# Reordering the first batch's attention steps ahead of the first FFN group

## The chip, the cores and the metric

The kernel runs on one NeuronCore of a Trainium2 chip. The metric is the device time of one launch in microseconds (us). Five runs of the kernel before are given, and one more execution was recorded by the hardware profiler. Engines are named as in the profile: PE (matmul), PEld (weight load), ACT, DVE, POOL (which also issues most loads), SP (which issues stores and DMA transposes).

## The reference

Two operations are fused. The first is a masked attention over `q`, `k`, `v` of shape 8 x 8 x 576 x 64 (batch, head, position, head dimension). The second is a feed-forward network with a squared ReLU on the 4608 x 512 result.

```python
scores = scale * np.matmul(q, k.transpose(0, 1, 3, 2))       # B=8, H=8, S=576, D=64
mask_plain = (rel >= 0) & (rel < 32)                          # heads 0..3
mask_dil = (rel >= 0) & (rel < 128) & (rel % 4 == 0)          # heads 4..7
attn = softmax(where(mask, scores, -1e9));  attn_out = attn @ v
x = attn_out.transpose(0, 2, 1, 3).reshape(4608, 512)
h = np.maximum(x @ w_in, 0.0)                                 # w_in 512 x 2048
out = (h * h) @ w_out                                         # w_out 2048 x 512
```

## The kernel before

**Data.** The order of work is written by hand (a manual schedule): each engine runs its instructions in the order in which the program issues them, and each instruction waits on semaphores for its operands and its buffers. Heads are handled in pairs e = 0..3. Pairs 0 and 1 have the plain window and pairs 2 and 3 the dilated one. The result of attention goes, transposed, into `xT`, whose four slabs (one per pair) are the four contraction tiles of the first FFN product. A batch of 576 tokens is cut into two parts for batches 0 and 1: part 0 is tokens 0 to 255, part 1 is tokens 256 to 575.

**FFN.** It runs in groups. The first 1024 tokens are in tiles of 256 tokens, the rest in tiles of 512. Every tile has groups of `w_in` products (PE line L665, then a Relu on ACT at L676 and a square on DVE at L677) and groups of `w_out` products (PE L700, then a copy on ACT at L706 and a store on SP at L639). `w_in` comes in four transfers of 512 columns each (in the text w_in 0 to w_in 3) and so does `w_out` (w_out 0 to w_out 3). POOL issues all of these. For the first tile, group 0 does the products of pairs 0 and 1 for two accumulators, group 1 the products of pairs 2 and 3 for the same two, and groups 2 and 3 use w_in 1.

**The order.** The string `PROGRAM` lists the attention steps. Everything ahead of its first `|` runs before FFN group 0, what stands between the first and the second `|` runs after group 0, and so on. A first-batch step is a letter, a pair and a part, and `first_step` carries it out:

- `T` transposes q and k of a pair on PE (L497, 8 instructions for q and 8 for k) into a PSUM tile of pool `ps_a`, which has two buffers.
- `C` copies that tile to SBUF (`xx`). For the plain pairs it is L511 for q and L512 for k; for the dilated pairs L504 for both and L506 for the rest of k. The last letter says which engine does L504 or L511: `a` is ACT, `v` is DVE; L506 and L512 are always on DVE.
- `B` and `S` are the bias and the score products (PE, L527 and L546) in a tile of pool `ps_f`, which has four buffers. The FFN accumulators use the same four.
- `E` is the exponential (ACT, L554), in part 1 followed by a mask multiplication (DVE, L557).
- `P` and `D` are the products with v (PE L584) and with ones (PE L600). Their results are in `ps_o` and `ps_d` (pair of tiles po and pd), in two tiles of `ps_f`, or in two of `ps_a`.
- `L` and `X` are the logarithm and the exponential of its negative on ACT (L607, L610), which make the reciprocal of the sum. `M` is the multiplication on DVE that writes `xT` (L617). In part 0, one L, X and M serve two pairs.
- `W`n is a run of n small products on zeros (PE L467), whose results nobody reads.

Steps with a leading `L` and a batch number (`L1:q00123`) issue loads on POOL; `z`, `y`, `u`, `m`, `n` and `h` are memsets, masks and a copy of v. Steps of later batches start with the batch number: `3k1` and `3q1` copy the transposed k and q of batch 3, pair 1, from `xx` (k on DVE at L252, q on ACT at L248), and `L3:x` issues the four DMA transposes (SP, L216) that fill `xx` for batch 3.

**What orders the queues.** POOL's loads are in program order, and an issue on POOL often waits for the landing of an earlier transfer. SP's queue holds stores and DMA transposes in program order as well.

Of the kernel before, what the change touches and what calls it, by code (L numbers as in the profile page):

```python
# [20 lines left out]
PROGRAM = (  # L21
    "L0:q001 L0:q023 L0:q101 L0:q123 L0:v0d L0:i0 L0:v1dr L0:i1 L0:v1p L0:i2 L0:i3 L0:o0 L0:o1 L0:o2 L0:o3 "
    "L1:q00123 z y L1:v0dp L1:q10123 L1:v1dpr w9 T00 C00a T10 C10a B00 B10 W2 S00 E00 B20 W1 S10 E10 u B30 W3 "
    "T20q W6 T20k C20v T30 C30v h W3 S20 E20 W2 S30 E30 T01 C01v T11 C11v W2 P00 P10 D00 D10 L00 X00 M00 P20 "
    "P30 D20 D30 L20 X20 M20 S01 T21 C21a T31 C31v E01 S11 E11 | S21 E21 | S31 E31 P21 P31 D21 D31 L21 X21 M21 "
    "L31 X31 M31 | | P01 P11 D01 D11 L01 X01 M01 L11 X11 M11 | | | | | | | | | | | | | m n | | | | | L2:q00123 "
    "L2:q10123 | 1q1 1q3 | 1q2 1k2 | 1k1 1v3 | 1a2 | 1v2 1k0 1q0 | 1o2 | 1a0 1a1 | 1k3 1o0 1o1 | 1a3 1Q0 | 1K0 "
    "1o3 | 1Q1 1K1 | 1Q2 | 1b0 | | 1Q3 1K2 L2:vwpdr L3:q00123 L3:q10123 | L2:x | | 2q0 | | 2k0 1V2 | 1b2 1p0 | "
# [847 lines left out]
```

## Time and profile before

| | us |
|---|---|
| median of 5 runs | 313.53 (313.09 to 316.47) |
| profiled execution | 313.28 |
| its span, first to last instruction | 311.5 |
| PE busy in the span | 302.0 (97%) |
| ACT busy | 197.3 (63%) |
| DVE busy | 195.5 (63%) |
| POOL busy | 93.8 (30%) |

The time of the profiled execution is 1.78 us more than its span. A timeline row gives start, duration, engine, line, operation, output and inputs, the count of merged instructions, and in brackets the idle time before it with what ended it. A row of a tile gives the durations as minimum, median and maximum, the first and last start, and below it the time from issue to landing of its DMAs. PE's records overlap, since matmuls are pipelined, so the time that a run of matmuls takes is read from the start of one row to the start of the next.

### The profile page before, as it was taken

To read this page: it belongs to the slowest core of one execution; us is meant where nothing else is said; L and a number is where in the kernel's file an instruction comes from. 1 tells how busy PE (TensorE), PEld (TensorE's weight loads), DVE (VectorE), ACT (ScalarE), POOL (GpSimd) and SP (SyncE) were. 2 spreads that over 40 slices of the span, in tenths; PEclk is the share of its full clock that TensorE was granted. 3 is DMA by queue.
4 is the path that set the end of the run, shared out by engine and by line. 5 is a ranking of instruction groups with operands and counts; after the bars stand their busy time and mean duration, and the time that the engine had idled before them with its cause. 6 is when DMAs were issued, how large, how long until landed. Compare 5 with 4: busy or idle time off the path is not lost.

```text
span 311.5 us, 6788 instructions
## 1 busy us (share of the span) xinstructions
PE 302.0 (97%) x2564; PEld 186.4 (60%) x2564; DVE 195.5 (63%) x637; ACT 197.3 (63%) x421; POOL 93.8 (30%) x138
## 2 busy tenths in 40 slices
PE   8889999999999999999999999999999999999994
PEld 3679746969755555555599555555555555445443
DVE  1456667998978879975798469946994234104400
ACT  6578538859878865795388547854786456226511
POOL 8689775464236255401451041000000000000000
PEclk9999999999999999999999999999999999999999
DMA  7999999999999979998799976502200210121022
GB/s 112 193 173 213 204 141 176 174 97 225 151 123 192 177 115 203 167 147 131 106 129 147 142 120 91 102 16 61 60 3 4 66 68 0 36 67 34 2 67 67
DMA packets 79808, 35.04 MB, mean 113 GB/s; under 512 B 49824, under 2 KB 74784, under 8 KB 79776
## 3 DMA queue, kind: packets, MB, share of 16 engines
q0 software_dynamic: 46592, 18.23, 51.7%
q1 hardware_dynamic: 32496, 16.06, 27.9%
q10 hardware_dynamic: 688, 0.33, 0.5%
q8 instruction: 20, 0.33, 0.4%
q14 instruction: 12, 0.10, 0.1%
HBM read 36.90 MB, written 9.44 MB: 149 GB/s over the span
## 4 chain that ended last, share of the span: by engine, by line
PE 84%; ACT 5%; DMA 4%; DVE 3%; POOL 2%; issue 2%; SPq 0%; ACTq 0%; POOLq 0%
PE pf L665 37%; PE pf L700 37%; PE po L413 3%; DMA w_in<-in_moe_w_in_dram 3%; PE pd L415 2%; PE pa L304 2%; ACT h2T L676 1%; PE pa L310 1%; ACT qT L248 1%; PE pa L235 1%; POOL qb L161 1%; POOL kb L161 1%; DMA out_dram<-osb 1%; DVE xT L428 1%; ACT rec L417 1%
## 5 line engine op out<-in xcount | busy, mean ns | idle before, releaser
L700 PE MATMUL pf<-w_out_sb,h2T 128*128 128x512 bf16 (+1 forms) x592 | 134.5, 373 | 0.5 <-ACT osb L706 0.5
L665 PE MATMUL pf<-xT,w_in 128*128 128x256 bf16 (+1 forms) x768 | 133.8, 326 | 1.0 <-DMA w_in<-in_moe_w_in_dram 0.4
L665 PEld LDWEIGHTS <-w_in 128*128 128x128 bf16 x768 | 82.3, 114 | 36.4 <-issue 1.2
L676 ACT ACTIVATE h2T<-pf 128x512 bf16<-128x512 f32 x144 | 83.6, 597 | 23.2 <-PE pf L665 22.6
L700 PEld LDWEIGHTS <-h2T 128*128 128x128 bf16 x592 | 54.3, 98 | 53.9 <-issue 0.7
L677 DVE TENSOR_TENSOR h2T<-h2T 128x512 bf16<-128x512 bf16 x144 | 58.0, 422 | 38.4 <-ACT h2T L676 36.7
L706 ACT COPY osb<-pf 128x512 f32<-128x512 f32 (+1 forms) x37 | 21.2, 572 | 43.6 <-PE pf L700 41.3
L428 DVE TENSOR_TENSOR xT<-po,rec 128x288 bf16<-128x288 f32 (+2 forms) x52 | 23.7, 456 | 31.5 <-ACT rec L418 31.1
L178 POOL DMA_DIRECT2D vbd<-in_v_dram x36 | 25.7, 729 | 45.9 <-PE pd L415 40.0
L417 ACT ACTIVATE rec<-pd 128x288 f32<-128x288 f32 (+2 forms) x52 | 21.5, 413 | 24.0 <-PE pd L415 22.9
L314 ACT ACTIVATE pt<-pa 128x352 bf16<-128x352 f32 (+6 forms) x56 | 27.6, 499 | 8.4 <-PE pa L310 4.7
L418 ACT ACTIVATE rec<-rec 128x288 f32<-128x288 f32 (+2 forms) x56 | 24.8, 444 | 1.8
L413 PEld LDWEIGHTS <-vbd 128*128 128x128 bf16 x286 | 16.8, 97 | 9.9 <-issue 0.7
L248 DVE COPY qT<-xx 64x288 bf16<-64x288 bf16 x80 | 19.6, 246 | 1.1
L191 POOL DMA_DIRECT2D vd<-in_v_dram x24 | 14.7, 621 | 15.3 <-DMA kb<-in_k_dram 8.7
L252 DVE COPY kbd<-xx 64x288 bf16<-64x288 bf16 x40 | 18.8, 470 | 0.6
L413 PE MATMUL po<-pt,vbd 128*128 128x96 bf16 (+3 forms) x263 | 18.0, 199 | 0.3 <-DVE vbd L207 0.2
L161 POOL DMA_DIRECT2D qb<-in_q_dram x18 | 12.9, 718 | 17.8 <-DMA xx<-qb 16.2
L415 PE MATMUL pd<-pt,mk 128*128 128x96 bf16 (+5 forms) x158 | 16.3, 204 | 0.0
L197 POOL DMA_DIRECT2D vbd<-in_v_dram x16 | 9.6, 603 | 13.0 <-PE pd L415 5.1
L161 POOL DMA_DIRECT2D kb<-in_k_dram x18 | 12.7, 707 | 0.8 <-DMA kb<-in_k_dram 0.5
L304 PE MATMUL pa<-qT,kbd 128*128 128x96 bf16 (+2 forms) x146 | 12.2, 201 | 0.5 <-ACT qT L248 0.5
(90 smaller groups left out, 234.3 us busy)
## 6 DMA issues: line engine op xcount, KB each, us to landing
out_dram<-osb SPq DMA_DIRECT2D x18, 128.0 KB, 2.7
qb<-in_q_dram POOLq DMA_DIRECT2D x7, 320.0 KB, 8.3
kb<-in_k_dram POOLq DMA_DIRECT2D x7, 320.0 KB, 10.1
vd<-in_v_dram POOLq DMA_DIRECT2D x32, 64.0 KB, 7.2
w_in<-in_moe_w_in_dram POOLq DMA_DIRECT2D x4, 512.0 KB, 7.4
w_out_sb<-in_moe_w_out_dram POOLq DMA_DIRECT2D x4, 512.0 KB, 12.4
qb<-in_q_dram POOLq DMA_DIRECT2D x7, 256.0 KB, 7.0
kb<-in_k_dram POOLq DMA_DIRECT2D x7, 256.0 KB, 8.2
```

The costliest lines, as they stand in the source:

```text
L161: nc.gpsimd.dma_start(t[0:n, part, hs, :], src[b, hs, t0 : t0 + RES * n, :].rearrange("h (p r) d -> p h (r d)", r=RES))
L178: nc.gpsimd.dma_start(dst[rows, e, i0:i1, rows], v[b, 2 * e + hl, 64 * i0 : 64 * i1, :].rearrange("(i p) d -> p i d", p=64),)
L248: copy(qT[rows, e, :, m0 : m0 + n].rearrange("p (c j) m -> p j c m", j=2)[:, jj, :, :], src)
L314: nc.scalar.activation(pt[:, off : off + n], ps[:, 0:n], ACT.Exp, scale=SCALE)
L413: nc.tensor.matmul(oo, vb[:, e, i, :], rh, start=(x == 0), stop=(x == len(mms) - 1), skip_group_check=True)
L417: nc.scalar.activation(rec[:, 0:n], d[:, 0:n], ACT.Ln)
L418: nc.scalar.activation(rec[:, 0:n], rec[:, 0:n], ACT.Exp, scale=-1.0)
L428: nc.vector.tensor_tensor(out=tok, in0=o if o is o3 else o[:, 0:n], in1=rec if o is o3 else rec[:, 0:n], op=ALU.mult)
L665: nc.tensor.matmul(acc[u][:, nt * x + y0 : nt * x + y1], w_in_sb[piece][:, kt, c0 : c0 + 509 : 4], xT[:, kt, t0 : t0 + y1 - y0], start=(kt ...
L676: nc.scalar.activation(hv, acc[u][:, :].rearrange("p (x n) -> p x n", x=per), ACT.Relu)
L677: nc.vector.tensor_tensor(out=hv, in0=hv, in1=hv, op=ALU.mult)
L700: nc.tensor.matmul(cur[m][:, c0:c1], h2[:, f, P * m : P * m + P], w_out_sb[:, f, c0:c1], start=(f == 0), stop=(f == NF - 1),)
```

## The change

Only `PROGRAM` changes. As a diff:

```
-    "T20q W6 T20k C20v T30 C30v h W3 S20 E20 W2 S30 E30 T01 C01v T11 C11v W2 P00 P10 D00 D10 L00 X00 M00 P20 "
-    "P30 D20 D30 L20 X20 M20 S01 T21 C21a T31 C31v E01 S11 E11 | S21 E21 | S31 E31 P21 P31 D21 D31 L21 X21 M21 "
+    "T20q W6 T20k C20v T30 C30v h W3 S20 E20 W2 S30 E30 T01 C01v T11 C11a W4 P00 P10 D00 D10 L00 T21 C21v T31 "
+    "C31v X00 M00 P20 P30 D20 D30 L20 X20 M20 S21 S31 E21 E31 S01 S11 E01 E11 | | P21 P31 D21 D31 L21 X21 M21 "
     "L31 X31 M31 | | P01 P11 D01 D11 L01 X01 M01 L11 X11 M11 | | | | | | | | | | | | | m n | | | | | L2:q00123 "
```

Step by step:

- `T21` and `T31`, the part-one transposes of the dilated pairs, move from behind `M20` to between `D10` and `P20`. `C21` goes from ACT to DVE. Both copies now stand ahead of `M00` and `M20` on DVE.
- `C11`'s L511 goes from DVE to ACT.
- Two zero products are added (`W2` becomes `W4`).
- The scores of part 1 are all issued ahead of group 0, dilated pairs first (`S21 S31`, then `S01 S11`), and so are their exponentials. In the kernel before, `S21` stood behind group 0 and `S31` behind group 1.
- `P21` and what follows it stay behind group 1, and `P01` behind group 3.

POOL's and SP's instructions and their order are the same in both kernels. PE has two more products (and their weight loads); ACT and DVE have the same work but for the two copies that change sides.

## The prediction

> **What bounds the kernel now.** I read the page's first part, then the chain of work that ended last, then the timelines of PE, ACT and DVE over the first 25 us, then the landings of the loads that the chain names. PE is busy nearly all the time:
>
> ```profile
> PE 302.0 (97%) x2564; PEld 186.4 (60%) x2564; DVE 195.5 (63%) x637; ACT 197.3 (63%) x421; POOL 93.8 (30%) x138
> ```
>
> So only 9.5 us of PE idle (311.5 - 302.0) can be won by reordering, and a reorder near the start pays only if PE stays earlier to the end. The chain in the stretch that changes (start, duration, what):
>
> ```profile
> 7.82 8.91 DMA w_in<-in_moe_w_in_dram
> ...
> 16.78 1.06 PE pf L665 x8
> 17.84 0.44 PE pf L546 x18
> 18.30 0.60 ACT pt L554
> 18.90 0.85 ACT h2T L676 x2
> 19.75 0.08 issue
> 19.82 0.61 ACT pt L554
> 20.44 0.02 issue
> 20.46 0.43 DVE pt L557
> 20.90 0.04 issue
> 20.94 0.59 PE pa L584 x14
> ```
>
> The reader is to see two limits. FFN group 0 cannot start before w_in 0 lands, at 7.82 + 8.91 = 16.73. Then S21 and E21, two Relus queued ahead on ACT, E31 and its mask come one after the other; P31 starts at 20.94 after 0.86 us of idle PE. Group 2 follows at 21.81.
>
> **The change part by part.** All PE times before 12.5 stay.
>
> *W4, C11.* Two zero products at 0.11 each (W2 took 12.53 to 12.75, into P00): P00 to D10 end 0.22 later, their last result at 13.77 instead of 13.55. C11's L511 (0.33) moves to ACT, idle from 11.3 to 13.58: nothing, and DVE is freed of it before L512.
>
> *T21, T31, C21, C31 early.* The transposes need the second q and k loads of the dilated pairs, which landed at 12.6 and 13.5 (issued at 5.0 and 5.7, 7.6 and 7.8 to landing), so PE runs them at 13.7 to 14.3 (0.15 for each 8). That is nearly free: before, PE waited there for v, whose two halves land at 13.8 and 14.3. P20 to D30 start at 14.3 (14.20 before) and their last result is out at 15.05. DVE does C21 from 14.2 (0.48 + 0.21, some 0.6 with overlap) and C31 to 15.3. ACT: L00 13.8, X00 to 15.05, L20, X20 to 16.3. M00 is now behind C31: 15.3 to 16.0 (before 14.87 to 15.56). M20 is 16.35 to 17.05 (before 16.28). If the k load were later, each 0.1 after 13.85 would be 0.1 on M00; it has 0.7 before 16.73.
>
> *All scores ahead of group 0.* S21 and S31 take 0.42 each (17.77 to 18.19 before): 14.98 to 15.8. S01 and S11 take 0.35 each, but need the two `ps_f` tiles that P00 and D00 held, so one waits for M00: 16.05 to 16.75. Group 0's two accumulators are then the tiles of S21 and S31, freed by E21 and E31. This is a new wait. ACT gets there at 16.3; one such exponential takes 0.60 and the next follows 0.51 later, so E21 is done at 16.9, E31 at 17.4, E01 and E11 at 17.9 and 18.4. Group 0 runs 16.9 to 17.9 in two halves, in place of 16.78 to 17.77. Behind this wait stands all of PE. Group 1 follows at once: 17.9 to 18.75, where before S21 stood between and it ran 18.19 to 19.18.
>
> *P21 to D31 with no stall.* Their masks are done by 17.9 on DVE, v landed at 17.8 (issued at 13.0, 4.8). They take 1.2 us: 18.75 to 20.0. Group 2 could start there, but needs w_in 1:
>
> ```profile
> L761 POOL DMA_DIRECT2D w_in<-in_moe_w_in_dram x1: 772/772/772, 13.7 to 13.7; - x1
> ...
> DMA to landing us min/median/max: 6.7/6.7/6.7
> ```
>
> It lands at 20.4 and no step here moves it. Group 2 starts at 20.45 instead of 21.81: **1.36 us won**, 0.45 us lost to the wait that is late next.
>
> *What comes later.* POOL's order is unchanged and its early waits are for transfers, so I hold the landings fixed and ask where PE meets them. w_in 2 (issued 18.3, 5.9) lands at 24.2; its group would come at 20.45 + 1.75 + 0.9 + 0.87 = 23.97, so it starts at 24.25 instead of 25.4: 1.15 left. w_out 3 (21.7, 16.2) lands at 37.9; its first products would come 1.15 before 39.25, at 38.1: just enough. The loads of batches 1 and 2 leave at least 0.5 more than this (the tightest: k of batch 2 lands at 61.8, its transposes move from 63.48 to 62.3). Then come the transposes of batch 3:
>
> ```profile
> L216 SPq DMA_TRANSPOSE xx<-qb x1: 3787/3787/3787, 84.4 to 84.4; - x1
> ...
> DMA to landing us min/median/max: 6.1/6.1/6.1
> ...
> 91.11 1.74 ACT L248 COPY qT<-xx 64x288 bf16<-64x288 bf16 x4
> ...
> 92.90 0.32 PE L304 MATMUL pa<-qT,kbd 128*128 128x96 bf16 x4 [0.45 <-ACT qT L248]
> ```
>
> The last lands at 84.4 + 6.1 = 90.5; step 3q1 copies it at 91.11 and PE is already waiting for that copy. Each step of that landing's past is a load: SP's transposes start at 74.70 when k lands (66.3 + 8.3), and POOL's issues back to 40 wait for landings. So 3q1 can come only 0.6 earlier, and 0.55 of PE's lead turns into idle: **0.6 us left**. The k copy 3k1 has less room (k lands at 80.2 + 9.5 = 89.7, copied at 89.86), but what follows it on DVE, the multiplication at 91.86, is wanted by PE only after 92.9. Beyond this PE has hardly any idle time to 307, and batch 4's copies (first at 112.03, k landed at 109.5) have 2.5 us of room.
>
> **Two rules against the change.** PE gets new gaps: 0.2 at 15.8, up to 0.15 at 16.75, 0.45 at 20, 0.5 more at 91. The granted clock by window (us, PE, PEld, DVE, ACT, POOL, clock, DMA):
>
> ```profile
> 20.00:21.00 1.00, 0.14 (x5) 0.16 (x6) 0.82 (x2) 0.43 (x1) 0.71 (x2) 1.00 1.22 94
> ```
>
> PE was idle 0.86 of this microsecond at clock 1.00. The Trainium skill, "TensorE: Matmul & The Clock Gate", section "A second HAM failure mode: psum-queue depth-cycling", says that frequent micro-idles between groups of matmuls make the clock swing between half and full. By it a gap could cost half of a 3.4 us window, 1.7 us (an estimate from that page); by the row nothing. I take the row, whose gap is larger than most of the new ones. The second: stores start about 1.1 us earlier (before, at 40.93), among the loads of batches 1 and 2. "DMA: Bandwidth & Descriptors", section "Queues, rings and completion order", says that each DMA engine takes turns between the queues that have work. By it the loads lose what stores gain: 1.1 us of output at 256 KB per 3.45 us of products is about 80 KB, at the 200 GB/s of the page's early slices 0.4 us on batch 3's landing, and 0.2 us of gain is left. By the row, loads are paced by their own landings and keep their times: 0.6. I take 0.6, since the bytes moved by then are the same.
>
> **Sum.** 313.28 - 0.6 = 312.7 for a profiled execution. The median of five is 0.25 above it, so the forecast is **312.9 us**. About 1% (3.1 us) is what a measurement of this kernel tells from no change.
>
> **The rivals.**
>
> - *The whole lead survives* (chance 0.2). Batch 3's transposes land earlier as well, because stores and some of POOL's waits on PE and DVE (0.8 at 54.0, 0.7 at 71.8) shift. For it: those waits. Against: the issues after 54.0 wait for loads again. 1.15 won: 312.4.
> - *Nothing is left* (0.2). The loads lose their 0.4 us to the earlier stores, or w_out 3 at 37.9 and the k copy on DVE take the rest: 0 to 0.2 won, 313.4.
> - *Slower* (0.15), by one mechanism: batch 3's last transpose. It took 6.1 us, the one before it 9.5 and the first 8.7. If the other order of stores and loads around it makes it 9.5 too, 3q1 starts at 84.4 + 9.5 = 93.9 at the earliest, against 91.1: 2.8 us slower, 316.3. It decides from a landing past 91.1, that is 0.6 late; one late by 1.5 costs 0.9 and gives 314.4. For it: PE already waits there. Against: the same bytes are moved, and the lead of 1.15 us does not help or hurt the landing.
> - *The new wait on E31* (within the slower case): it takes PE's place on the chain at 17.4, and costs the whole gain only if it is 1.8 us later.
>
> **How the numbers follow.** The forecast's case has 0.45, with 312.9 (its own range 312.6 to 313.2). The range reaches from the whole lead with the 0.4 us spread of most runs below it, 311.9, to a landing 1.5 late, 314.4. The bulk of the worst cases and a lucky double gain lie outside. Over 1% faster would need 3.1 us, more than twice what the first 25 us can give: 0.03. Over 1% slower needs a landing 3.7 us late or a clock that drops twice: 0.07. Within 1%: 0.90.
>
> **What would show it.** Right: P31 without idle time ahead of it, group 2 at 20.4 with a short wait for w_in, the w_out products starting at about 33.8, and a wait of about 1 us for 3q1 with PE resuming at 92.3. Wrong: group 0 after 17.5; an idle PE at 38; a granted clock under 1.00 in the first 25 us; batch 3's q landing later than 91; or PE's lead at 100 being more than 1 us.

## The result

The changed kernel takes 313.4 us (median of 44 runs, 312.25 to 315.24) against 314.04 us for the kernel before on the same chip (79 runs, 312.54 to 317.63). The measured ratio is 0.9967, with a 95% interval of 0.9951 to 0.9983, which is about 1.0 us faster (the medians lie 0.64 us apart, the means 1.15 us). Three later measurements of unchanged copies gave 0.9956 [0.9932, 0.9980] and 0.9955 [0.9932, 0.9978] for the kernel after, and 1.0008 [0.9980, 1.0036] for the kernel before. Executions more than 1.5% above the fastest of their kernel (a few of the kernel before, at most one of any other) are left out of the ratios and of the counts and medians by clock below.

### The profile after

The execution profiled with these runs took 313.63 us (span 311.9, granted clock 0.999), so it is no faster than the profiled execution of before (313.28). The page's first part, then PE's timeline over the stretch that changed (start, duration, what; in brackets the idle time before it and what ended it):

```profile
PE 301.8 (97%) x2566; PEld 186.3 (60%) x2566; DVE 196.5 (63%) x637; ACT 197.2 (63%) x421; POOL 93.9 (30%) x138
```

```profile
16.55 1.96 PE L665 MATMUL pf<-xT,w_in 128*128 128x256 bf16 x16 [0.43 <-ACT pt L554]
...
18.96 0.46 PE L584 MATMUL pa<-pt,vd 64*64 64x32 bf16 x16
...
19.96 1.94 PE L665 MATMUL pf<-xT,w_in 128*128 128x256 bf16 x16
...
25.55 0.63 PE L665 MATMUL pf<-xT,w_in 128*128 128x256 bf16 x4 [1.88 <-DMA w_in<-in_moe_w_in_dram]
```

The rows of the kernel before that these and the later ones are compared with (group 2, the products of w_in 1 and 2, the first `w_out` products and the last run of them):

```profile
21.81 1.92 PE L665 MATMUL pf<-xT,w_in 128*128 128x256 bf16 x16
...
24.46 10.65 PE L665 MATMUL pf<-xT,w_in 128*128 128x256 bf16 x96
34.94 2.32 PE L700 MATMUL pf<-w_out_sb,h2T 128*128 128x512 bf16 x10
...
305.93 1.91 PE L700 MATMUL pf<-w_out_sb,h2T 128*128 128x256 bf16 x16 [0.50 <-ACT osb L706]
```

The new wait for the exponentials is there (0.43 ahead of group 0). P31 (second row of after) has no idle time ahead of it. Group 2 starts at 19.96, 1.85 us earlier than before (21.81). Then, after one more group of products, PE stands still for 1.88 us, and the products of w_in 2 start at 25.55, where before, eight products of 0.87 us behind the start at 24.46, they came at 25.33: the whole lead is gone. The row of POOL's loads says why (issue time, and below it the time to landing, of w_in 1 and of w_in 2):

```profile
L761 POOL DMA_DIRECT2D w_in<-in_moe_w_in_dram x1: 772/772/772, 13.5 to 13.5; - x1
...
DMA to landing us min/median/max: 6.4/6.4/6.4
...
L761 POOL DMA_DIRECT2D w_in<-in_moe_w_in_dram x1: 797/797/797, 17.9 to 17.9; - x1
...
DMA to landing us min/median/max: 7.6/7.6/7.6
```

w_in 1 landed at 19.9 and stopped nobody; w_in 2 landed at 25.5, and the products that need it start there. The last of batch 3's transposes (its tile's row), and the timelines of ACT and PE around the copy 3q1:

```profile
L216 SPq DMA_TRANSPOSE xx<-qb x1: 3569/3569/3569, 82.5 to 82.5; - x1
...
DMA to landing us min/median/max: 7.3/7.3/7.3
```

```profile
90.32 0.33 PE L415 MATMUL pd<-pt,mk 128*128 128x192 bf16 x3
...
90.69 0.41 ACT L417 ACTIVATE rec<-pd 128x288 f32<-128x288 f32 x1 [0.75 <-DVE kbd L252]
91.13 0.44 ACT L418 ACTIVATE rec<-rec 128x288 f32<-128x288 f32 x1
91.48 1.74 ACT L248 COPY qT<-xx 64x288 bf16<-64x288 bf16 x4
...
93.27 0.32 PE L304 MATMUL pa<-qT,kbd 128*128 128x96 bf16 x4 [0.45 <-ACT qT L248]
```

The last transpose is in at 82.5 + 7.3 = 89.8, but the copy starts at 91.48. ACT gets to it only then: it comes right behind L417 and L418, and L417 had waited for 0.75 us. The row names DVE's copy 3k1 (L252) as what ended this wait. But L417 reads `pd`, which L415 on PE had finished at 90.32 + 0.33 = 90.65, just ahead of 90.69 (in `r_after2` 88.98 and 89.02), and it does not read what L252 writes. So it most likely waited for PE's own sums, and PE lists no idle time from 86.6 to there. The copy's time then follows PE's.

A profile of a second copy, `r_after2`, belongs to an execution that ended 1.3 us earlier than the profiled one of before (311.98 us, span 310.2, clock 1.000):

```profile
20.32 1.92 PE L665 MATMUL pf<-xT,w_in 128*128 128x256 bf16 x16
...
33.46 3.83 PE L700 MATMUL pf<-w_out_sb,h2T 128*128 128x512 bf16 x17
...
91.60 0.32 PE L304 MATMUL pa<-qT,kbd 128*128 128x96 bf16 x4 [0.45 <-ACT qT L248]
...
304.62 1.91 PE L700 MATMUL pf<-w_out_sb,h2T 128*128 128x256 bf16 x16 [0.50 <-ACT osb L706]
```

Its w_in 2 landed at 23.3. No wait for it follows, and of the lead of 1.49 us at group 2 all but 0.2 us is carried on: the `w_out` products start at 33.46 (before 34.94), 3q1's product at 91.60 (92.90), and the last run of `w_out` products at 304.62 (305.93). So one program gives different courses. These two reach group 2 within 0.4 us of each other, and w_in 2's landing decides between them.

Behind this stretch all executions that were profiled run alike. From the first of the `w_out` products to the last run of them it is 270.99 us in the profile of before, 271.10 in the first one of after and 271.16 in `r_after2`. Over all 14 profiles, the experiments' included, it is 270.96 to 271.57 us, while the first `w_out` product lies anywhere from 33.46 to 37.73. What an execution has won or lost by then stays to the end, within 0.6 us.

### Two parts of the gain

Each execution, profiled or not, lists its mean granted clock (but for the 79 runs of before above, which have none on record and are not in the table). Sorting by it separates the runs of the kernel before into two heaps. The line at 0.9965 was drawn after seeing them. The stays at half clock that profiles show below last 3.4 or 6.8 us; of 313 us, half of that makes a mean of 0.995 or 0.989. Means of 0.997 to 0.999 need no such stay: in the profiles of after (0.999) and `e_after_w1` (0.997) the only windows under 1.00 lie behind the last product.

| kernel | executions | with a dropped clock | median of these | median of the others | mean of all |
|---|---|---|---|---|---|
| before | 219 | 100 (46%) | 315.85 | 313.44 | 314.55 |
| after | 87 | 16 (18%) | 313.97 | 312.86 | 313.25 |

- **With the clock held**, after is faster by 313.44 - 312.86 = 0.58 us (95% from resampling the runs: 0.25 to 0.85). By the means of the same executions it is 0.41 us (0.21 to 0.60).
- **Dropped clocks** are rarer and cheaper. Before, such an execution loses 2.4 us, in 46% of cases; after, 1.1 us, in 18%. Of the means' difference of 1.3 us (1.0 to 1.55), 0.4 is the first part and the remaining 0.9 this one.

### The profile page after: what moved, and what is told of

Its sections match the earlier page's. It is cut to its first block, busy times and chain, and to the rows that moved or that the text cites. A ratio compares the mean times of both kernels' runs of the same rounds, so it can differ in the third digit from the quotient of the medians.

```text
span 311.9 us, 6795 instructions
## 1 busy us (share of the span) xinstructions
PE 301.8 (97%) x2566; PEld 186.3 (60%) x2566; DVE 196.5 (63%) x637; ACT 197.2 (63%) x421; POOL 93.9 (30%) x138
## 4 chain that ended last, share of the span: by engine, by line
PE 69%; DMA 22%; POOL 4%; issue 2%; ACT 2%; DVE 0%; ACTq 0%; POOLq 0%
PE pf L700 32%; PE pf L665 30%; DMA kb<-in_k_dram 12%; DMA vbd<-in_v_dram 3%; DMA w_in<-in_moe_w_in_dram 3%; PE po L413 3%; PE pd L415 2%; DMA vd<-in_v_dram 2%; DMA qb<-in_q_dram 2%; PE pa L304 1%; POOL qb L161 1%; PE pa L310 1%; POOL w_out_sb L766 1%; POOL vbd L178 1%; POOL kb L161 1%
## 5 line engine op out<-in xcount | busy, mean ns | idle before, releaser
L676 ACT ACTIVATE h2T<-pf 128x512 bf16<-128x512 f32 x144 | 83.6, 597 | 25.5 <-PE pf L665 24.9
L417 ACT ACTIVATE rec<-pd 128x288 f32<-128x288 f32 (+2 forms) x52 | 21.5, 413 | 24.0 <-PE pd L415 22.9
L418 ACT ACTIVATE rec<-rec 128x288 f32<-128x288 f32 (+2 forms) x56 | 24.8, 444 | 1.8
L252 DVE COPY kbd<-xx 64x288 bf16<-64x288 bf16 x40 | 18.8, 470 | 0.6
L415 PE MATMUL pd<-pt,mk 128*128 128x96 bf16 (+5 forms) x158 | 16.3, 203 | 0.0
L304 PE MATMUL pa<-qT,kbd 128*128 128x96 bf16 (+2 forms) x146 | 12.2, 201 | 0.5 <-ACT qT L248 0.5
```

The lines of the kernel that those rows point to most:

```text
L415: nc.tensor.matmul(dd, ones[:, :], rh, start=(x == 0), stop=(x == len(dms) - 1), skip_group_check=True)
L417: nc.scalar.activation(rec[:, 0:n], d[:, 0:n], ACT.Ln)
L418: nc.scalar.activation(rec[:, 0:n], rec[:, 0:n], ACT.Exp, scale=-1.0)
L676: nc.scalar.activation(hv, acc[u][:, :].rearrange("p (x n) -> p x n", x=per), ACT.Relu)
```

## The experiments

The kernels were measured in three sets, each on one chip with the kernel before beside it (the ratios are to that). **The loads' theory** (A in the recorded expectations): PE's lead lives or dies with the landings of early loads, above all w_in 2, which vary from execution to execution. Its rivals: batch 3's transposes take the lead, as forecast (B); or the new order itself delays w_in 2 (C). The granted clocks of the first set brought in **the clock's theory** (D): the times differ because the clock drops less often. The later sets test it.

### Unchanged copies: r_before, r_after, r_after2

> The kernel before once more, for a second profile of it. Theory A: w_in 2 lands anywhere from 24.2 to 25.5 here too, mostly without a wait, because PE asks for it only at 25.3. Theory C: it lands at about 24.2 again, clearly ahead of the changed kernel. Time: ratio 1.00.

> The changed kernel once more, for a second profile of it. In its first profile PE reaches group 2 at 19.96 (before: 21.81), asks for w_in 2 at 23.5 and waits 1.88 us for its landing at 25.5, so it starts group 4 at 25.55, later than the kernel before (25.33). Theory A (the landing of w_in 2 sets PE's pace at 25 us and varies from execution to execution): group 2 again near 20.0 to 20.5, and a wait for w_in 2 whose length differs, from 0.3 us (a landing at 24.2 as in the profile of before) to 1.9 us; time about 1.0 us under the kernel before. Theory B (the transposes of batch 3 at 90 us cut the lead): a lead at 25 us that is larger than the lead at 95 us. Theory C (the change itself delays w_in 2, for instance because DVE and ACT now work beside POOL's issues): w_in 2 lands at 25.5 again.

> The changed kernel on the same chip as the last three, to compare with. Theory D: 15 to 25% low-clock executions, full-clock median about 0.6 us under that of the kernel before, all executions together about 1.0 to 1.3 us under it.

The profile of `r_before` fell into an execution with a dropped clock (316.6 us, clock 0.989). PE's timeline:

```profile
12.30 0.48 PE L600 MATMUL pf<-pt,mk 128*128 128x96 bf16 x8
14.84 0.26 PE L584 MATMUL po<-pt,vd 64*64 64x64 bf16 x1 [2.06 <-DMA vd<-in_v_dram]
...
18.49 1.89 PE L665 MATMUL pf<-xT,w_in 128*128 128x256 bf16 x8
20.31 0.69 PE L546 MATMUL pf<-xx 64*64 64x32 bf16 x16
```

and the same stretch by windows (start and end, length, busy share of PE, PEld, DVE, ACT and POOL with their counts, granted clock, DMA share, GB/s):

```profile
13.00:14.00 1.00, 0.00 (x0) 0.00 (x0) 0.30 (x1) 0.97 (x2) 0.71 (x1) 1.00 1.21 197
14.00:15.00 1.00, 0.16 (x1) 0.12 (x1) 0.69 (x1) 0.07 (x1) 0.06 (x1) 0.60 1.29 196
15.00:16.00 1.00, 1.00 (x18) 0.63 (x17) 0.00 (x0) 0.00 (x0) 0.91 (x2) 0.50 1.37 167
...
20.00:21.00 1.00, 1.00 (x21) 0.61 (x20) 0.00 (x0) 0.00 (x0) 0.91 (x3) 0.50 1.10 69
21.00:22.00 1.00, 1.00 (x12) 0.80 (x11) 0.28 (x1) 0.91 (x2) 0.87 (x2) 0.99 1.23 174
```

PE stands idle for 2.06 us in front of P20, waiting for v. At 14.2 the granted clock falls to 0.50 and stays there until 21.0. Eight products of group 0 take 1.82 us (18.49 to 20.31), against 0.99 in the profiled execution of before. This is the place where the change puts `T21` and `T31`. In the first profile of after the same stretch is full of products:

```profile
13.00:14.00 1.00, 1.00 (x43) 0.89 (x41) 0.37 (x2) 0.60 (x2) 0.57 (x2) 1.00 1.24 203
14.00:15.00 1.00, 1.00 (x40) 0.75 (x40) 0.97 (x5) 0.87 (x2) 1.00 (x3) 1.00 1.30 203
```

And in `r_after2`, where PE still stood 0.73 us in the midst of P20's and P30's products, no longer gap was formed, and the clock stayed at 1.00.

`r_after` (313.0 us median; its profile is of an execution of 314.06 us at clock 0.998) is the slowest of the three profiles of after:

```profile
17.57 1.96 PE L665 MATMUL pf<-xT,w_in 128*128 128x256 bf16 x16 [0.65 <-ACT pt L554]
...
26.11 9.80 PE L665 MATMUL pf<-xT,w_in 128*128 128x256 bf16 x88 [1.11 <-DMA w_in<-in_moe_w_in_dram]
```

Its group 2 starts at 20.85, a lead of 0.96 us, and a pause of 0.29 us follows within it, which the profile ties to no other instruction. Then w_in 2 landed at 26.1, and its products came 0.78 us later than before.

### w_in 2 taken away: e_after_w1, e_before_w1

```
 in the w_in products of the first tile
+    if tk0 == 0 and 8 <= f < 12:
+        f -= 4
```

The two groups that need w_in 2 take columns of w_in 1 in its place, so the products with w_in 2 are left out for the first 256 tokens. The transfer itself is still made.

> The changed kernel, but groups 4 and 5 of the first tile take the columns of w_in 1 in place of those of w_in 2 (so 512 columns of the first 256 tokens are computed with other weights); the transfer itself is still made. Nothing then waits for w_in 2 before 27 us. Theory A: no idle PE from 20 to 28 us and PE's lead over the kernel before at 30 us about 1.8 us; the time 1.0 to 1.8 us under the kernel before, and below the changed kernel by up to 1 us if nothing later takes it back. Theory B: PE is ahead by 1.8 us at 85 us, and by at most 0.6 to 1.0 us at 95 us, with a longer wait for step 3q1. If w_in 2 is not what limits, the time is that of the changed kernel.

> The kernel before with the same edit (groups 4 and 5 of the first tile take the columns of w_in 1). Theory A: no wait is removed where w_in 2 lands ahead of 25.3, so 0 to 0.3 us faster. If it is faster by 1 us or more, w_in 2 was a limit of the kernel before as well, in executions that its profile does not show.

On the kernel after, the ratio is 0.9958 [0.9938, 0.9978]; the median with the clock held is 312.55 us, 0.1 to 0.3 under those of after (312.65 in the same set, 312.86 over all; the 95% intervals, -0.3 to 0.7 and -0.1 to 0.7, take in zero). On the kernel before it is 0.9978 [0.9953, 1.0003], and 313.36 with the clock held, against 313.44: nothing that can be told from none. The profile of `e_after_w1`, PE's timeline (its lines stand two lower than in the kernel after):

```profile
20.59 2.08 PE L667 MATMUL pf<-xT,w_in 128*128 128x256 bf16 x16
...
23.41 10.65 PE L667 MATMUL pf<-xT,w_in 128*128 128x256 bf16 x96
33.90 2.32 PE L702 MATMUL pf<-w_out_sb,h2T 128*128 128x512 bf16 x9
```

There is no idle time from 20 to 33, and the `w_out` products start 1.0 us earlier than before. So the wait for w_in 2 is a limit, of the kernel after only as far as the profiles show, and in a part of its executions. Its removal wins at most some 0.3 us in the median, which is not clear of nothing: either it seldom costs the whole lead, or other early waits take its place. These runs do not tell which. That the new order delays w_in 2 has no support: it landed at 24.2, 24.7 and 25.6 in three profiles with the order of before, at 25.5, 26.1, 23.3 and 24.7 in four with the order of after. Each spread is wider than the difference of their means (24.8 and 24.9).

### Either half alone: p_trans, p_scores

`p_trans` is the kernel after with the scores in their old places, `p_scores` the kernel before with the scores moved ahead:

```
 p_trans, from after
-M20 S21 S31 E21 E31 S01 S11 E01 E11 | | P21
+M20 S01 E01 S11 E11 | S21 E21 | S31 E31 P21
 p_scores, from before
-C31v E01 S11 E11 | S21 E21 | S31 E31 P21
+C31v S21 S31 E21 E31 S11 E01 E11 | | P21
```

> Only the first half of the change: T21, T31 and their copies between the products of part one, C11 on ACT, W4; scores and exponentials of part two stand where they stood in the kernel before. Theory D (part of the gain is the clock: early PE gaps of 1 to 2 us, in which PE waits for k or v of the first batch, drop the granted clock to 0.5 for some 6 us in about half of the executions of the kernel before, which costs 2 to 2.5 us there; the transposes fill that gap): low-clock executions (mean granted clock under 0.9965) fall from about 47% to about 20%, as in the whole change, which alone is 0.6 us on the mean; at full clock the time is that of the kernel before, because the stall of 0.86 us ahead of P31 is still there. Ratio about 0.998. Theory A alone (only the stall ahead of P31 and the landing of w_in 2 matter): ratio 1.000, low-clock share unchanged.

> Only the second half: all scores and exponentials of part two ahead of FFN group 0, with the transposes, copies and W2 where they were in the kernel before. Theory A: the stall ahead of P31 goes, group 2 at about 20.5 to 21.0, and the time at full clock is 0.4 to 0.7 us under the kernel before, as in the whole change. Theory D: the gap ahead of P20 is not filled, so low-clock executions stay near 47%. Ratio about 0.998.

| kernel | ratio | with a dropped clock | median of the others |
|---|---|---|---|
| p_trans | 0.9992 [0.9964, 1.0020] | 1 of 14 | 313.40 |
| p_scores | 1.0033 [1.0006, 1.0060] | 16 of 21 | 313.34 (5 executions) |

The transposes alone keep the clock up (before in the same set: 16 of 49 dropped) and win nothing where the clock holds (313.40 against 313.46). Their own profile warns against too simple a rule. T21's k came late there, and PE stood still for 1.29 us in the midst of the transposes, yet the clock stayed at 1.00:

```profile
15.60 0.34 PE L497 MATMUL pa<-mk,kb 80*64 80x80 bf16 x8 [1.29 <-DMA kb<-in_k_dram]
```

```profile
14.00:15.00 1.00, 0.31 (x10) 0.19 (x8) 0.00 (x0) 0.89 (x2) 0.00 (x0) 1.00 1.24 193
15.00:16.00 1.00, 0.40 (x22) 0.41 (x24) 0.03 (x1) 0.34 (x1) 0.16 (x1) 1.00 1.26 148
```

The scores alone make the kernel **slower**, by little: the interval lies just above 1, and 16 of 21 executions have a dropped clock. The profile of `p_scores` shows how, in PE's timeline and by windows:

```profile
16.74 0.69 PE L546 MATMUL pf<-xx 64*64 64x32 bf16 x16 [0.88 <-ACT xx L504]
```

```profile
16.00:17.00 1.00, 0.26 (x10) 0.26 (x11) 0.86 (x3) 0.69 (x2) 0.13 (x1) 0.69 1.37 183
17.00:18.00 1.00, 1.00 (x37) 0.93 (x34) 0.50 (x2) 0.48 (x1) 1.00 (x2) 0.50 1.26 202
...
22.00:23.00 1.00, 1.00 (x24) 0.81 (x25) 0.57 (x2) 0.60 (x1) 1.00 (x2) 0.50 1.24 205
```

Neither half came out as expected: about 0.998 had been forecast for each. With the transposes still late, `S21` now comes right behind them and PE waits 0.88 us for the copy `C21`, which is on ACT behind `L20` and `X20`. In this execution the clock goes to half in that gap, at 16.4, and stays there for 6.8 us. Group 0 runs through the middle of it. With the transposes early, that gap is not there in any profile of after. The early transposes thus make the early scores affordable: they fill one gap, and keep another from forming.

### Gaps filled with products on zeros: b_fill, s_fill, a_fill, a_fill2

```
 b_fill, from before;  s_fill, the same from p_scores
-D10 L00
+D10 W9 L00
 a_fill, from after
-T01 C01v
+T01q W6 T01k C01v
 a_fill2, from a_fill
-C31v X00
+C31v W4 X00
```

> The kernel before with nine more products on zeros (1.0 us of PE) between D10 and P20, where PE waits for v. Theory D: the filler keeps the clock, so low-clock executions fall from about 47% to under 25%, and the mean falls by 0.5 us or more, though PE does more work; at full clock the time is the same or up to 0.2 us longer. Without theory D the filler can only cost: ratio 1.000 to 1.001, low-clock share unchanged.

> Only the second half of the change (all scores ahead of group 0, 17 low-clock executions of 22), with nine more products on zeros between D10 and P20. Theory D: the transposes of the first half do their work for the clock as filler, so any filler in their place serves: low-clock executions fall from 77% to under 25% and the mean by 1 us or more. If the share stays above 50%, the drop comes from the new gap behind the transposes (0.9 us ahead of S21, waiting for the copy of C31), which the filler does not cover.

> The changed kernel with six more products on zeros (0.65 us) between the transposes of q and of k of pair 0, part one, where PE waits 0.4 to 1.1 us for k in all profiles. Theory D: the remaining low-clock executions (14 of 66) become fewer, under 10%, and the mean falls by 0.1 to 0.3 us; at full clock the same as the changed kernel within 0.2 us. Against it: if the gap that drops the clock is another one, the share stays at about 20%.

> The changed kernel with filler at two places: six products on zeros between q's and k's transposes of pair 0, part one, and four (0.44 us) ahead of P20. Theory D: low-clock executions at or under 7% (with the first filler alone: 1 of 14). The second filler costs up to 0.4 us where v has landed early, most of it hidden by the wait for E31. At full clock 312.8 to 313.2.

| kernel | ratio | with a dropped clock | median of the others |
|---|---|---|---|
| b_fill | 0.9991 [0.9962, 1.0021] | 1 of 14 | 313.66 |
| s_fill | 1.0006 [0.9979, 1.0034] | 12 of 21 | 313.83 |
| a_fill | 0.9982 [0.9957, 1.0007] | 1 of 14 | 312.83 |
| a_fill2 | 0.9970 [0.9950, 0.9991] | 0 of 22 | 313.11 |

`b_fill` is the plainest test of the clock's theory: nothing but nine products on zeros in the gap in front of P20. 1 of 14 executions has a dropped clock, against 16 of 49 of the kernel before in the same set and 46% over all. Fourteen are few: chance alone would give such a difference in about one case in eleven. Together with `p_trans` (2 of 28) it is about one in eighty (Fisher's exact test), and `a_fill` in the same set shows 1 of 14 too. The ratio of `b_fill`, 0.9991, is not clear of 1, so that its time falls with its drops is not shown. Its profile caught the one execution that dropped, and shows that another gap can do it as well:

```profile
12.01 0.34 PE L497 MATMUL pa<-mk,kb 80*64 80x80 bf16 x8 [0.69 <-DMA kb<-in_k_dram]
```

```profile
11.00:12.00 1.00, 0.32 (x8) 0.20 (x8) 0.46 (x1) 0.35 (x1) 0.59 (x1) 1.00 1.44 192
...
13.00:14.00 1.00, 1.00 (x15) 0.95 (x13) 0.74 (x3) 0.00 (x0) 0.59 (x1) 0.50 1.29 216
...
15.00:16.00 1.00, 1.00 (x7) 0.61 (x5) 0.25 (x1) 0.69 (x2) 0.24 (x2) 0.59 1.33 159
16.00:17.00 1.00, 0.85 (x22) 0.48 (x20) 0.44 (x1) 0.00 (x0) 1.00 (x2) 1.00 1.25 131
```

PE waited 0.69 us for k there, and the clock is at half from 12.4, that is 0.4 us after the gap's end, to 15.8. The filler itself ran inside this stretch, and the clock was back before P20. It was one stay of some 3.4 us where `r_before` had twice that; whether the filler cut it short is one profile and no test.

`s_fill` fills P20's gap in `p_scores`; 12 of 21 still drop, so P20's gap is not what does it there. The gap of 0.88 us in front of `S21`, where the drop in `p_scores` began, is the one left that `b_fill`, with its 1 of 14, does not have. That it does it is argued from this, not tested: no run filled that gap alone. The own profile of `s_fill` has that gap at clock 1.00 (span 310.9, clock 0.999):

```profile
16.56 0.46 PE L546 MATMUL pf<-xx 64*64 64x32 bf16 x16 [0.88 <-ACT xx L504]
```

The same gap of the same length drops the clock in one execution and not in another. `a_fill` and `a_fill2` have a dropped clock in 1 of 14 and 0 of 22 executions, against 16 of 87 of after. But beside `a_fill2`, `r_after2` had only 2 of 22, so it is not shown that the fillers keep out the last drops. Nor do they gain time: `r_after2` had 0.9955, and the intervals overlap.

### A version with both ideas: a_best

```
 from a_fill
-E21 E31 S01 S11 E01 E11 | | P21
+E21 E31 | S01 S11 E01 E11 | P21
```

> The changed kernel with the filler of six between q's and k's transposes, and with the scores of the plain pairs behind group 0 instead of ahead of it. Group 0 then takes the accumulators that P00 and D00 held, and no longer waits for E21 and E31 (0.4 to 0.65 us in the profiles). Theory A: group 0 starts right behind S31 or at w_in 0's landing, group 2 up to 0.5 us earlier than in the changed kernel, or at w_in 1's landing; the time is 0 to 0.4 us under the changed kernel, because w_in 1 and w_in 2 hold PE next. Low-clock executions as with the first filler, under 15%.

0.9972 [0.9947, 0.9998], 1 of 22 with a dropped clock, 313.28 with the clock held. Group 0 no longer waits for an exponential:

```profile
16.99 1.06 PE L665 MATMUL pf<-xT,w_in 128*128 128x256 bf16 x8 [0.31 <-DMA w_in<-in_moe_w_in_dram]
```

It waits for w_in 0 in its place, and the time is no better than after's. In the profiled execution a pause of 1.14 us just ahead of group 2, tied to no other instruction, took what was won. No complete version that was tried beats the kernel after.

## Why the prediction was right, and where it was not

The forecast was 312.9 us, and 313.4 was measured. Its gain of 0.6 us agrees with the medians of the executions whose clock holds (0.58). Of its steps, those up to group 2 agree in the main with what was measured. Those on w_in 2, on batch 3's transposes and on the clock do not, and the last of these missed more than half of the gain in the mean (0.9 of 1.3 us).

- **Group 0 waits for E21 and E31: right.** 0.43 us of wait in the first profile, 0.65 in `r_after2` and `r_after`; starts at 16.55, 17.04 and 17.57, forecast 16.9. The last is past 17.5, which was named as a sign of being wrong.
- **P31's stall goes: right.** No idle time ahead of it in any of the three profiles of after.
- **Group 2 waits for w_in 1 and starts at 20.45: right in size, not in cause.** Starts at 19.96, 20.32 and 20.85, with no wait for w_in 1 in any; it landed at 19.9 in the first. The won time was sized at 1.36 and measured 1.85, 1.49 and 0.96. All of these are against the one profile of before at full clock.
- **w_in 2 at 24.2 leaves 1.15: a size that does not exist.** One profile gave 24.2. The landings of unchanged programs lie from 23.3 to 26.1, so what is left of the lead is anything from all of it (`r_after2`) to less than none (the first profile and `r_after`, 0.22 and 0.78 us behind). The sum also has 25.4 for a start that the rows put at 25.33.
- **Batch 3's transposes leave 0.6: wrong.** I took 90.5 and 91.11 to be the same event with 0.6 of room. The landing of the last transpose and the copy 3q1 lie from 0.6 to 7.0 us apart (`b_fill`: 86.1 and 93.15), yet the wait of 0.45 at L304 is in all 14 profiles. In the first profile of after the copy had been free to start for 1.7 us. It is thus not the transposes': the copy starts when ACT comes to it, behind L417 and L418, and L417 most likely waits for PE's own sums. ACT comes there earlier when PE does, so a lead passes through: 1.30 of 1.49 us in `r_after2`. That the gain still came out near 0.6 is luck, two errors cancelling: this cap was not there, and w_in 2 took its place in part of the executions.
- **The clock: wrong.** The row shown there was one microsecond with a gap at clock 1.00, and I let it outweigh the rule of the Trainium skill ("TensorE: Matmul & The Clock Gate", section "A second HAM failure mode: psum-queue depth-cycling"), that micro-idles between groups of matmuls make the clock swing between half and full. The rule held in this kernel, in a part of the executions: in four profiles the clock went to 0.50 in or behind gaps of 0.69 to 2.06 us, for 3.4 or 6.8 us. I had also weighed it from the wrong side: I asked what new gaps the change makes, not which old one it fills. The profile of before was taken at clock 1.000, in one of the executions that kept it, so no row of it could show the cost. The five times could have given a hint: one was 316.47 beside 313.09. Its clock is not on record, but all 45 executions of before in the table that took over 316 us had a dropped clock.
- **Stores among the loads: not tested.** No run moved the stores by themselves. But in `r_after2`, where the first came 1.5 us earlier (39.45 against 40.93), only 0.2 us of the lead was lost between the first `w_out` product and the last run, so they cost no more than this there.

Of the rivals, the whole lead survives in single executions, and so does nothing of it. The slower one, a late transpose of batch 3, was not seen: the landings of after were at 89.8, 90.5 and 87.9 in the three profiles.

**Open.** No profile caught a dropped clock in the kernel after, so which of its gaps does it in 16 of 87 executions is not shown. Why the same gap drops the clock in one execution and not in another is not shown either. Executions over 314 us with the clock held (11 of 71 of after, 11 of 119 of before) have other causes. The profile of `p_trans` shows some: at 315.26 us and clock 1.000, it waited 0.84 and 1.29 us for k and 0.81 us for w_in 0. `p_scores` kept its clock in 5 executions only, so what the early scores are worth by themselves is known poorly. And whether the batch 3 transposes would bind at all with a larger lead was not tried.

## What to carry to other kernels

Look at the spread of the times before the profile: where a few runs lie 1% above the rest, one profile shows one of two courses, and the first question is which. A short PE gap early in a kernel can cost far more than its own length, because it may halve the clock for the several microseconds behind it; useful work that is put into such a gap is worth more than its duration, and an edit that opens one (as the scores alone did) costs more. A cap that is read from two times lying close together holds only if their distance stays the same in a second execution. And where a row names what ended a wait, look whether the waiting instruction reads what the named one writes.

## What the hardware did that I had not expected

- In four profiles the granted clock went to 0.50. In `r_before` (gap of 2.06 us) and `p_scores` (0.88 us) it fell within the gap and stayed for 6.8 us. In `b_fill` it fell 0.4 us behind a gap of 0.69 us and stayed for 3.4 us. In `e_before_w1` it fell at 14.0, within a gap of 0.29 us and 1.7 us behind one of 1.26 us, and stayed for 6.8 us. The length of a gap alone does not decide it: gaps of 0.82 us (the profile of before), 0.88 us (`s_fill`), 1.14 us (`a_best`) and 1.29 us (`p_trans`) passed at clock 1.00.
- Nine products on zeros in one gap, about 1 us of PE's time (0.11 each), left a dropped clock in 1 of 14 executions where 16 of 49 had it without them, and cost some 0.2 us where the clock held (313.66 against 313.46; the interval, -0.04 to 0.48, takes in zero).
- The landing of the same load varied by 2.8 us between three executions of the kernel after (23.3 to 26.1 for w_in 2, issued at 17.7 to 18.3). This is more than everything the change won.
